# A long chain of engines issued from a written-out table: another order, found with a plan in which TensorE's instruction packets queue behind transfers

## The chip, the cores and the metric

The kernel runs on one core of a Trainium2 chip. The core has five engines that each work through their own list of instructions in order: PE (TensorE, matmuls; its weight loads are listed apart as PEld and overlap the matmuls), DVE (VectorE), ACT (ScalarE), POOL (GpSimd) and SP (SyncE, which here only issues transfers). They wait for one another through semaphores. Sixteen DMA engines carry the transfers. PE writes to PSUM, the others move results from there to SBUF, the on-chip memory; such a move is called an evacuation below. The metric is the device time of one execution in microseconds (us).

## The reference, cut to what matters

One sequence of 2048 positions with 512 channels goes through a state-space layer and an MLP, each with a layernorm ahead and a residual.

```python
def ssm(u, A_re, A_im, B_re, B_im, C_re, C_im, log_dt, Dskip):   # D = 512, N = 128, L = 2048
    dt = exp(log_dt)[:, None]
    logdA = dt * (A_re + 1j * A_im)
    P = exp(logdA[:, :, None] * arange(L))
    K = einsum("dn,dnl,dn->dl", C, P, dt * B).real               # the kernel of the convolution
    y = irfft(rfft(u padded to 2L) * rfft(K padded to 2L))[:L]   # along L, for each channel
    return y + u * Dskip

h  = x + ssm(layernorm(x), ...)
h2 = h + B(layernorm(h))   # B(z) = gelu(layernorm(z) @ w1 + b1) @ w2 + b2
```

B begins with a layernorm of its own; w1 is 512 x 1376 and w2 1376 x 512.

## The kernel before, in words

*The work.* The convolution's K is never formed by L exponentials for each state. Positions are split into blocks, so that K is a product of a table of powers within a block and one across blocks. Both tables come from the parameters by small sums on DVE and POOL, by exponentials and sines on ACT, and by long DVE products:

- The head: loads of the parameters and of u, transposes (L776 to L814), `split` and `restack` (L758 to L765; the transfers `ar<-ar` of 64 KB on SP), the exponentials of `bexps` (L800) and `aexps` (matmuls L1014, ACT L1018). One ACT_TABLE_LOAD (L559) then turns ACT from exponentials to sines.
- The chain: PE makes angles (L1070), ACT their sines (L1074), and DVE multiplies them into the tables (L1081 to L1083, L1089, L1090, and the large products L1041). The layernorm of u is beside it: BN_STATS on DVE (L947, four for each group of rows), and `unorm` (L959).
- K, in two halves: `kgen` (L1115, L1116) is 1024 tiny matmuls, 128x33, that read the tables. The second half reads the products that the chain ends with. A carry of a few rows between neighbouring blocks goes by four transfers on SP (L1136). `kspec` (L1159) takes the K blocks to spectra, which ACT or DVE evacuates.
- The way through memory: the spectra are stored to DRAM (`AK_d<-ar`, 512 KB each, eight of them, called at L1174) and loaded back in another layout (`ar<-AK_d`, eight of 512 KB, L1178), all on SP's queue through the helper `dma` (L577). `fstage` (L991) takes them a stage further on PE. `xspec` (L971) and `fstage` do the same for the input, with no trip through memory.
- `inverse`: products of the spectra (L1207, L1212; DVE or POOL) and matmuls back (L1223); its results are turned by DMA transposes (`turn`, L1229).
- `lead` and `tail` (L1285 to L1350): residual, skip term, the layernorms of the MLP.
- `mlp`: w1 and gelu (PE L1372, ACT L1374), w2 and the output (PE L1394, DVE L1396), and stores of the output. `load_mlp` (L1253 to L1257) loads the weights, `load_small` (L1260 to L1268) the bias b1, as 128x10 and 96x1 single values, and Dskip.

*What sets the order.* Each of 966 pieces of work is only recorded, by `Sched.add`, with what it reads and writes, its costs and the engines that may do it (the evacuations, several sums, the inverse's products and `unorm` have two: ACT or DVE, DVE or POOL). `Sched.run` then goes through the table `ORDER`, 966 numbers written out in the code, and issues the pieces one after the other; a negative number stands for a piece's second engine. So the table sets each engine's order and the choice of engine. While it goes, `run` keeps a plan of times. In this kernel the plan has two effects on what is issued: which of the four PSUM buffers (128x1024 f32) a piece gets, and where filler matmuls (L1488, work without a use) stand, which are put in where the plan sees PE wait. 78 of them are issued.

*Packets in the plan.* PE's instructions come to it in packets, and the plan's class `Ring` holds the transfers under way. At each 256th instruction of PE, `until` says when the next packet has come: before, 3.65 us after the last, and longer by 0.3 of the time in which transfers were under way. The numbers in the plan are the planner's own and no measurement.

Lines of the new kernel are 8 higher than these from L280 on: its L1123 is L1115 here, L1049 is L1041, L955 is L947, L585 is L577, L575 is L567.

Of the kernel before, what the change touches and what calls it, by code (L numbers as in the profile page):

```python
# [15 lines left out]
P = 128  # L16
# [147 lines left out]
class VS(V):  # L164
# [49 lines left out]
]  # L214


FREE = {"PE": 1.3, "ACT": 0.7, "DVE": 0.8, "POOL": 1.4, "SP": 0.7}
WIN, PHASE, ACTIVE = 3.4133, -1.4, 1.25
SWITCH = 0.095


class Clock:
    def __init__(self):
        self.end, self.act, self.warm = PHASE + WIN, 0.0, False

# [31 lines left out]
class Ring:  # L257
# [3 lines left out]
    def add(self, x, y):  # L261
        if y <= x:
            return
# [6 lines left out]
    def until(self, t0):  # L270
        o = 0.0
# [1258 lines left out]
```

## Time and profile before

| what | value |
|---|---|
| three runs | 240.89, 238.55, 242.34 us |
| median | 240.89 us |
| the profiled execution | 238.77 us |
| its span, first to last instruction | 237.0 us |
| mean granted clock of PE | 0.993 |
| DMA | 24.16 MB in 42294 packets |

A row of the profile gives an engine, a line, an operation with its tiles (`ar` is SBUF, `ps` PSUM, `AK_d` the spectra in DRAM, `in_...` the inputs), a count, and busy time. Behind `<-` stands what ended an idle time: an engine with its last operation, a DMA, or `issue`, where the engine waited for nothing that the profile shows. In rows of the timeline the first number is the start, the second the length, and a wait ahead of the row is in brackets. Rows of the list of waits give the sum, the count, and the longest. SPq is SP issuing a transfer. A queue's row gives packets, MB and its share of the time of 16 DMA engines; q8 carries PE's instructions and q1 the kernel's own transfers.

### The profile page before, as it was taken

What the parts mean: (1) busy time and instruction counts of PE and PEld (TensorE: products, weight loads), DVE (VectorE), ACT (ScalarE), POOL (GpSimd) and SP (SyncE); (2) the same over time, 40 slices, a digit from 0 to 9 for tenths busy, and PEclk for the clock granted to TensorE, in tenths of its full rate; (3) what the DMA queues carried; (4) which work ended last, traced back from release to release, by engine and by line L of the source; (5) the groups of instructions that cost most, each with busy time, mean ns of one, the idle gap of its engine ahead of it and who ended that gap; (6) DMA issues with size and microseconds to landing.
All of it is one profiled execution on the core that took longest, in us unless ns stands there. A gap on an engine that the chain in (4) does not pass through costs nothing.

```text
span 237.0 us, 7873 instructions
## 1 busy us (share of the span) xinstructions
PE 208.3 (88%) x3375; PEld 119.2 (50%) x3386; DVE 173.6 (73%) x325; ACT 170.9 (72%) x208; POOL 44.8 (19%) x216
## 2 busy tenths in 40 slices
PE   5195899869998899769999978999999999999993
PEld 3033743426776567445766554565444444444443
DVE  3999898999999875448989978998934757122022
ACT  6998999899999797539989968978547305604700
POOL 6854930000000033008060001601000101000000
PEclk9999799999999999999999999999999999999999
DMA  6972010100000448805898899340933051611203
GB/s 163 222 147 68 25 49 0 47 1 6 3 6 11 116 141 200 301 17 160 265 224 212 223 202 307 68 89 3 175 58 67 3 100 44 144 25 33 55 22 78
DMA packets 42294, 24.16 MB, mean 102 GB/s; under 512 B 25810, under 2 KB 39604, under 8 KB 42260
## 3 DMA queue, kind: packets, MB, share of 16 engines
q1 hardware_dynamic: 41810, 23.34, 41.0%
q8 instruction: 26, 0.43, 0.7%
q10 hardware_dynamic: 450, 0.33, 0.4%
q14 instruction: 8, 0.07, 0.1%
HBM read 9.90 MB, written 6.29 MB: 68 GB/s over the span
## 4 chain that ended last, share of the span: by engine, by line
PE 50%; DVE 17%; ACT 16%; DMA 9%; issue 4%; SPq 2%; ACTq 1%; DVEq 0%
PE ps L1394 16%; PE ps L1372 16%; DMA ar<-AK_d 4%; ACT ar L565 4%; PE ps L991 4%; DVE ar L1041 3%; ACT ar L1018 3%; PE ps L971 3%; ACT ar L800 3%; PE ps L1159 3%; DMA ar<-ar 2%; DVE ar L1081 2%; PE ps L1115 2%; PE ps L1116 2%; PE ps L1223 2%
## 5 line engine op out<-in xcount | busy, mean ns | idle before, releaser
L565 ACT CAST ar<-ps 128x1024 bf16<-128x1024 f32 (+2 forms) x71 | 63.9, 976 | 19.0 <-PE ps L991 5.3
L1374 ACT ACTIVATE ar<-ps,ar 128x512 bf16<-128x512 f32 (+1 forms) x44 | 28.6, 686 | 28.0 <-PE ps L1372 19.2
L1372 PE MATMUL ps<-ar 128*128 128x512 bf16 (+2 forms) x192 | 39.9, 361 | 0.1
L1394 PE MATMUL ps<-ar 128*128 128x512 bf16 (+3 forms) x181 | 39.1, 366 | 0.3
L1074 ACT ACTIVATE ar<-ps 128x1024 bf16<-128x1024 int16 x36 | 34.6, 1047 | 1.8 <-PE ps L1070 1.1
L567 DVE CAST ar<-ps 128x1024 bf16<-128x1024 f32 (+2 forms) x21 | 24.3, 1172 | 13.3 <-PE ps L991 6.8
L1396 DVE TENSOR_TENSOR ar<-ps,ar 128x512 bf16<-128x512 f32 (+1 forms) x17 | 11.0, 657 | 28.5 <-PE ps L1394 28.3
L1372 PEld LDWEIGHTS <-ar 128*128 128x128 bf16 (+1 forms) x192 | 18.8, 100 | 19.4 <-issue 1.2
L1394 PEld LDWEIGHTS <-ar 128*128 128x128 bf16 (+1 forms) x187 | 18.0, 98 | 19.9 <-issue 0.4
L1207 DVE TENSOR_TENSOR ar<-ar 128x2048 bf16<-128x2048 bf16 x21 | 25.4, 1243 | 1.0 <-PE ps L1223 0.9
L1488 PE MATMUL ps<-ar 128*128 128x512 bf16 x73 | 20.5, 419 | 5.8 <-DMA ar<-in_A_u_dram 4.8
L1070 PE MATMUL ps<-ar 128*32 128x512 f16 (+1 forms) x368 | 21.6, 331 | 3.9 <-ACT ar L1074 3.9
L1116 PE MATMUL ps<-ar 128*20 128x33 bf16 x512 | 20.9, 248 | 3.7 <-issue 3.7
L1115 PEld LDWEIGHTS <-ar 128*20 128x20 bf16 x512 | 18.4, 123 | 5.0 <-issue 3.5
L1115 PE MATMUL ps<-ar 128*20 128x33 bf16 x512 | 20.8, 248 | 0.0
L991 PE MATMUL ps<-ar 128*32 128x256 bf16 (+1 forms) x384 | 18.2, 309 | 2.9 <-DMA ar<-AK_d 2.0
L1116 PEld LDWEIGHTS <-ar 128*20 128x20 bf16 x512 | 18.2, 124 | 2.1 <-issue 1.6
L927 POOL TENSOR_TENSOR ar<-ar 128x4 f32<-128x4 f32 (+1 forms) x5 | 5.7, 1145 | 67.9 <-DVE ar L616 58.7
L971 PE MATMUL ps<-ar 128*32 128x512 bf16 x256 | 17.3, 380 | 0.0
L1041 DVE TENSOR_TENSOR ar<-ar 128x2048 bf16<-128x2048 bf16 x14 | 16.2, 1219 | 0.0
L1488 PEld LDWEIGHTS <-ar 128*128 128x128 bf16 x78 | 7.7, 105 | 16.4 <-issue 5.4
L1070 PEld LDWEIGHTS <-ar 128*32 128x32 f16 x368 | 9.9, 98 | 12.0 <-issue 9.3
(113 smaller groups left out, 295.9 us busy)
## 6 DMA issues: line engine op xcount, KB each, us to landing
AK_d<-ar SPq DMA_DIRECT2D x8, 512.0 KB
ar<-AK_d SPq DMA_DIRECT2D x8, 512.0 KB
ar<-in_A_u_dram SPq DMA_DIRECT2D x4, 512.0 KB
out_dram<-ar SPq DMA_DIRECT2D x30, 64.0 KB
ar<-in_B_w_dram SPq DMA_DIRECT2D x4, 344.0 KB
ar<-ar SPq DMA_DIRECT2D x20, 64.0 KB
ar<-in_B_w_dram SPq DMA_DIRECT2D x2, 640.0 KB
ar<-ar SPq DMA_DIRECT2D x8, 48.0 KB
```

The costliest lines, as they stand in the source:

```text
L565: act.copy(out_fn(), in_fn())
L971: pe.matmul(pst(p)[32 * cg:32 * cg + 32, 512 * z:512 * z + 512], lhsT=BD.ap()[:, 32 * f + 2 - 2 * jl:32 * f + 34 - 2 * jl], rhs=un[2 * (2 ...
L991: pe.matmul(pst(p)[64 * h + z:64 * h + z + 32, w * (k + r):w * (k + r) + w], lhsT=T.ap()[:, f, r, z:z + 32], rhs=rhs(f), start=True, stop= ...
L1070: pe.matmul(pst(p)[32 * g:32 * g + 32, 256 * j:256 * (j + n)].rearrange("p (a b) -> p a b", a=n), lhsT=W2[DELTAS.index(d)].ap(), rhs=S2[g] ...
L1074: add("ACT", c_act(1024), lambda e, o_=o_, i_=i_: act.activation(o_(), i_(), ACT.Sin, scale=SINSC), r=[p, TBL], w=[sc[cs]])
L1115: pe.matmul(o, lhsT=Ar.ap()[:, :, d], rhs=Br.ap()[:, :, d], start=True, stop=False, tile_position=(0, 32 * g))
L1116: pe.matmul(o, lhsT=Ai.ap()[:, :, d], rhs=Bi.ap()[:, :, d], start=False, stop=True, tile_position=(0, 32 * g))
L1207: (dve if e == "DVE" else gp).tensor_tensor(pieces(o).rearrange("p z (a r d) -> p a z r d", a=4, r=2), k, x, ALU.mult)
L1372: pe.matmul(pst(p)[:fs, 512 * z + 128 * t0:512 * z + 128 * t1], lhsT=w1s[dc].ap()[:, fc * P:fc * P + fs], rhs=ybuf.ap().rearrange("p (t c) ...
L1374: add("ACT", c_act(512, 1), lambda e, p=p, z=z, fc=fc, fs=fs: act.activation(hT.ap()[:fs, fc, :], pst(p)[:fs, 512 * z:512 * z + 512], ACT. ...
L1394: pe.matmul(pst(p)[:, 512 * z + c0:512 * z + c1], lhsT=hT.ap()[:fs, fc, 128 * t:128 * t + 128], rhs=w2s[fc].ap()[:fs, c0:c1], start=(fc == ...
L1488: pe.matmul(slots[z][:, 0:512], lhsT=identb.ap(), rhs=hs[15].ap(), start=True, stop=True)
```

## The change

The table `ORDER` is another permutation of the same 966 pieces, with other choices of engine for some 60 of them; what each piece computes and what it depends on is unchanged. The plan's model of packets is new, and so the fillers are 66 instead of 78, and some PSUM buffers are others. The pieces that moved, as far as the prediction speaks of them:

- DVE: the last four of the 16 BN_STATS of the input's layernorm stand behind the chain's last product instead of ahead of the chain. A net two of the inverse's products (L1207), a net one of the `unorm` and two scalings go from DVE to POOL; one sum (`den`) comes from POOL; memsets are exchanged between the two, and evacuations between DVE and ACT, both ways.
- PE: the second half of K begins with other groups, and two groups of `kspec` (L1159) that read the carry stand behind the first of them instead of ahead. One group of the inverse (L1223) stands ahead of the first matmul of the MLP.
- SP: the 128x10 bias load stands among the restacks of the head instead of ahead of the first AK_d loads; the four first AK_d stores follow in a row; the AK_d loads stand apart, with stores, a slice of w1 (344 KB), w2's last rows (96 KB) and the carry between them; the last AK_d load stands behind four turns instead of three.

SP's order in the head now, around the bias load:

```order
L1273 DMA ar<-in_A_Dskip_dram 1x4x32
L585 DMA ar<-ar 64x1x512 x2
L1273 DMA ar<-in_B_b_dram 128x10x1
L585 DMA ar<-ar 64x1x512 x4
L1273 DMA ar<-in_A_Dskip_dram 1x4x32 x2
L1144 DMA ar<-ar 12x2048 x4
```

Before, all four Dskip loads came last, behind the restacks and ahead of the carry, and the bias load as the prediction shows it. The diff, with the table cut to a line:

```diff
 ORDER = [
...
 ]
@@
+CUT, EARLY = 0.2, 0.4
@@ class Ring:
     def __init__(self):
-        self.q = [[-100.0, -100.0] for _ in range(6)]
-    def add(self, x, y):
-        if y <= x:
-            return
-        for q in self.q:
-            if q[0] - 0.02 <= x <= q[1] + 0.02:
-                q[1] = max(q[1], y)
-                return
-        min(self.q, key=lambda q: q[1])[:] = [x, y]
-    def until(self, t0):
-        o = 0.0
-        for a, b in self.q:
-            o += max(0.0, min(b, t0 + 5.5) - max(a, t0))
-        return t0 + 3.65 + 0.3 * min(o, 5.5)
+        self.q = []
+    def add(self, a, b, turn):
+        self.q = [(a, b, turn)] + self.q[:9]
+    def until(self, t0, q=None):
+        f = t0 + 1.15
+        for a, b, turn in self.q if q is None else q:
+            if turn:
+                if a < t0 and b > f:
+                    f = max(f, min(b, t0 + 2.05))
+            elif a < t0 - CUT and b - EARLY > f:
+                f = b - EARLY
+        return f + 2.45
+    def late(self, t0, blk):
+        a, b, turn = self.q[0]
+        f = self.until(t0, self.q[:1])
+        return max(0.0, f - blk) if f > t0 + 3.6 else 0.0
@@ Sched.run, a piece of PE
                 while n0 < ipe:
-                    n1 = min(ipe, n0 - (n0 - 192) % 256 + 256)
+                    n1 = min(ipe, n0 - (n0 - 177) % 256 + 256)
                     t = clk.work(t, c * (n1 - n0) / o.ni, o.act / o.cost[0])
                     n0 = n1
-                    if (n1 - 192) % 256 == 0:
-                        t = blk = max(t, ring.until(blk))
+                    if (n1 - 177) % 256 == 0:
+                        t = max(t, ring.until(blk))
+                        blk0, blk = blk, t
@@ Sched.run, a transfer
-                ring.add(a, dma_busy)
+                    ring.add(end, dma_busy, False)
+                d = ring.late(blk0, blk)
+                free["PE"] += d
+                blk += d
@@ load_small
-        add("SP", 0.55, lambda e: nd(b1_bf.ap()[:, 0:10], B_b1[0:1280].rearrange("(fc p) -> p fc", p=P)), w=[b1_bf], byts=8192)
-        add("SP", 0.55, lambda e: nd(b1_bf.ap()[0:96, 10:11], B_b1[1280:1376].rearrange("(p o) -> p o", o=1)), w=[b1_bf], byts=8192)
+        add("SP", 0.6, lambda e: nd(b1_bf.ap()[:, 0:10], B_b1[0:1280].rearrange("(fc p) -> p fc", p=P)), w=[b1_bf], byts=400000)
+        add("SP", 0.55, lambda e: nd(b1_bf.ap()[0:96, 10:11], B_b1[1280:1376].rearrange("(p o) -> p o", o=1)), w=[b1_bf], byts=30000)
```

In the new plan a packet goes out 1.15 us after the last boundary, but behind transfers already issued, takes 2.45 us, and a transfer that is issued later can still delay it (`late`). The bias loads stand in the plan with more bytes, since their values are single; what they load is the same.

More of the change, by code (lines that the diff above doesn't have):

```diff
@@ L328, in run @@
         dma_busy, bulk, ring = 0.0, 4.0, Ring()
-        ipe, blk, md, pst, issued, held = 0, -10.0, 0, 0.0, 0.0, 0.0
+        ipe, blk, blk0, md, pst, issued, held = 0, -10.0, -20.0, 0, 0.0, 0.0, 0.0
         order, seen = [], set()
@@ L396, in run @@
                 bulk = share(a, o.byts / 230e3, dma_busy)
-                ring.add(a, bulk)
+                ring.add(end, bulk, False)
                 o.end = bulk + 0.3
@@ L405, in run @@
                     dma_busy = max(share(end, 2.5, bulk), dma_busy)
+                    ring.add(end - c, dma_busy, True)
                 else:
```

67 rows, old and new, of the table ORDER are left out of this document.

## The prediction

> **What bounds the kernel now.** I read the page first: busy time by engine, the DMA queues, the chain of work that ended last.
>
> ```profile
> PE 208.3 (88%) x3375; PEld 119.2 (50%) x3386; DVE 173.6 (73%) x325; ACT 170.9 (72%) x208; POOL 44.8 (19%) x216
> ```
>
> PE (TensorE) is the busiest, but an 88% share is a mean over stages. So the second view cuts the span where the work changes. The columns are the length, the busy time with the number of instructions for PE, PEld, DVE, ACT and POOL, the granted clock, the busy share of the DMA engines and GB/s.
>
> ```profile
> 36.00:82.00 46.00, 40.20 (x1051) 24.67 (x1044) 44.39 (x92) 43.29 (x51) 0.13 (x1) 1.00 0.10 24
> 82.00:99.70 17.70, 16.88 (x601) 11.92 (x592) 9.89 (x18) 12.64 (x13) 4.37 (x6) 1.00 0.70 201
> 99.70:102.60 2.90, 0.12 (x7) 0.05 (x8) 1.24 (x2) 1.01 (x1) 0.00 (x0) 1.00 0.27 102
> 102.60:134.40 31.80, 30.99 (x817) 20.90 (x816) 28.42 (x28) 28.39 (x31) 9.43 (x4) 1.00 0.75 185
> 134.40:150.50 16.10, 13.40 (x196) 7.85 (x193) 14.04 (x27) 13.16 (x17) 1.45 (x2) 1.00 0.99 249
> 150.50:233.50 83.00, 82.51 (x487) 40.26 (x491) 44.27 (x85) 39.66 (x57) 6.67 (x4) 1.00 0.30 62
> ```
>
> From 36 to 82 us DVE has 44.4 of 46 us: it is the bound, with ACT (43.3) close behind. From 82 on PE is, except in the hole at 99.7. In 134.4 to 150.5 every DMA engine is busy (0.99). The MLP after 150.5 is PE alone, 82.5 of 83.0.
>
> The third view is the waits of PE from 82 to 151 us, with what ended them; the fourth the timeline at the two ends that matter.
>
> ```profile
> PE ps L1116 <- issue: 2.8, 1, 2.8
> PE ps L991 <- DMA ar<-AK_d: 2.0, 2, 1.6
> PE ps L991 <- issue: 0.8, 1, 0.8
> PE ps L1320 <- ACT ar L565: 0.3, 1, 0.3
> ```
> ```profile
> 34.60 1.28 ACT L559 ACT_TABLE_LOAD   x1
> 75.48 5.77 DVE L1041 TENSOR_TENSOR ar<-ar 128x2048 bf16<-128x2048 bf16 x5
> 81.19 1.05 PE L1159 MATMUL ps<-ar 32*128 32x256 bf16 x31 [0.78 <-DMA ar<-ar]
> 82.17 0.27 PE L1115 MATMUL ps<-ar 128*20 128x33 bf16 x4
> 102.55 0.23 PE L1116 MATMUL ps<-ar 128*20 128x33 bf16 x1 [2.78 <-issue]
> 150.96 0.60 PE L1372 MATMUL ps<-ar 128*128 128x256 bf16 x4
> ```
>
> DVE's last chain products end at 75.48 + 5.77 = 81.25; 0.92 later, at 82.17, PE begins the second half of the kernel's K, which reads them. In 82 to 151 PE waits 2.8 + 0.8 = 3.6 us for "issue", which is neither data nor a buffer.
>
> **What the issue waits are.** The page counts 26 packets of the instruction queue, 0.43 MB, and PE's two rows 3375 + 3386 = 6761 instructions: 260 for each packet, so a packet carries about 256. Now the DMA view of two stretches around the hole, and PE's rate and stall in a stretch without traffic.
>
> ```profile
> q8 instruction: 26, 0.43, 0.7%
> ```
> ```profile
> q1 hardware_dynamic: 488, 1.79, 92.1%
> ```
> ```profile
> q1 hardware_dynamic: 57, 0.18, 19.3%
> q8 instruction: 1, 0.02, 2.5%
> ```
> ```profile
> 88.01 1.93 SPq L1265 DMA_DIRECT2D ar<-in_B_b_dram  x1
> 90.06 0.70 SPq L577 DMA_DIRECT2D AK_d<-ar  x1
> 90.93 4.44 SPq L577 DMA_DIRECT2D ar<-AK_d  x4
> ```
> ```profile
> 68.00:72.00 4.00, 4.00 (x170) 3.47 (x173) 4.00 (x10) 3.49 (x5) 0.00 (x0) 1.00 0.02 4
> 90.00:92.00 2.00, 2.00 (x55) 1.21 (x49) 0.72 (x3) 1.03 (x2) 0.87 (x1) 1.00 0.55 64
> ```
> ```profile
> 73.29 0.25 PE L1116 MATMUL ps<-ar 128*20 128x33 bf16 x1 [0.91 <-issue]
> ```
>
> In 94 to 100 us (the first of the two) the only queue with packets is the kernel's data, at 92%: no packet of instructions in 6 us. In 100 to 102.5 (the second) one comes, as the data thins out, and PE goes on at 102.55. The data are the four AK_d loads issued in a row from 90.93 to 95.37, 2 MB. The bias load of 1280 values issued at 88.01 delayed them: in 90 to 92 the engines moved 64 GB/s at a share of 0.55. The stall at 72.4 (0.91) is of another kind: DMA share 0.02 ahead of it, but 343 instructions in 4 us, 256 in 3.0. So there are two limits, a packet that queues behind transfers and a rate of packets.
>
> [...]
>
> **The change, part by part.** *DVE ahead of the chain.* The order of DVE (VectorE) before, at the end of the head; BN_STATS are statistics of input rows, L1081 (later) the chain:
>
> ```order
> L616 TENSOR_SCALAR ar<-ar 128x16
> L947 BN_STATS ar<-ar 128x6 x3
> L755 TENSOR_TENSOR ar<-ar 128x512
> L616 TENSOR_SCALAR ar<-ar 128x16
> L947 BN_STATS ar<-ar 128x6
> L626 TENSOR_TENSOR ar<-ar 128x8
> L733 TENSOR_SCALAR ar<-ar 64x32
> ```
>
> The order of DVE now, at the end of the chain; L1049 are its products, L955 the same BN_STATS, L575 evacuations:
>
> ```order
> L624 TENSOR_SCALAR ar<-ar 128x16
> L634 TENSOR_TENSOR ar<-ar 128x512
> L1049 TENSOR_TENSOR ar<-ar 128x2x2x512 x2
> L575 CAST ar<-ps_66 128x4x256
> L955 BN_STATS ar<-ar 128x6
> L575 CAST ar<-ps_65 128x2x8x64
> L955 BN_STATS ar<-ar 128x6 x2
> L575 CAST ar<-ps_65 128x2x8x64
> L955 BN_STATS ar<-ar 128x6
> ```
>
> Four BN_STATS moved from ahead of the chain to behind its last product. Their row (28 to 36 us) and those of the evacuations:
>
> ```profile
> L947 DVE BATCH_NORM_STATS2 ar<-ar 128x6 f32<-128x512 bf16 x6 | 3.8, 682 | 0.0
> L567 DVE CAST ar<-ps 128x1024 bf16<-128x1024 f32 (+2 forms) x21 | 24.3, 1172 | 13.3 <-PE ps L991 6.8
> L565 ACT CAST ar<-ps 128x1024 bf16<-128x1024 f32 (+2 forms) x71 | 63.9, 976 | 19.0 <-PE ps L991 5.3
> ```
>
> 3.8 / 6 = 0.63 each, 2.5 us off a saturated engine. Other exchanges ahead of the chain's end nearly cancel: one evacuation (1.17) leaves DVE, another comes, two small sums and a scaling come, memsets leave. I take 0.5 more, partly through the table load at 34.60 coming earlier. The chain's end moves by -3.0, to 78.25, and the K start to 79.2. Bounds: -1.0, if ACT, which has 46 - 43.3 = 2.7 us idle in this stretch and little of it at the end, sets the chain; -3.5.
>
> *PE after the chain.* Now the tiny K matmuls of the second half come first; the two L1159 groups of 16 that waited for the carry (0.78) follow. From 82.17 to 134.4 PE took 52.2 us, of it 2.78 + 0.82 + 0.34 (the smaller AK_d wait, 2.0 - 1.6) and 0.3 waits: 48.0 work. The L1159 groups add 1.2 (L1159's row above, 1.05 for 31, and the next start); of the L971 pairs three go ahead of the chain's end and two come behind it, which I cost at nothing together. 49.2 then.
>
> *The transfers.* SP's order before, around AK_d (the K spectra's way through memory; L1136 is the carry):
>
> ```order
> L1136 DMA ar<-ar 12x2048 x4
> L577 DMA AK_d_69<-ar 128x8x256 x2
> L577 DMA AK_d_68<-ar 128x8x256
> L577 DMA ar<-in_B_w_dram 96x512
> L1265 DMA ar<-in_B_b_dram 128x10x1
> L577 DMA AK_d_68<-ar 128x8x256
> L577 DMA ar<-AK_d_69 128x2048
> L577 DMA ar<-AK_d_68 128x2048 x2
> L577 DMA ar<-AK_d_69 128x2048
> L1136 DMA ar<-ar 12x2048 x4
> ```
>
> and now:
>
> ```order
> L1144 DMA ar<-ar 12x2048 x4
> L585 DMA AK_d_69<-ar 128x8x256
> L585 DMA AK_d_68<-ar 128x8x256 x2
> L585 DMA AK_d_69<-ar 128x8x256
> L585 DMA ar<-AK_d_68 128x2048
> L585 DMA ar<-in_B_w_dram 96x512
> L585 DMA ar<-AK_d_69 128x2048
> L585 DMA ar<-in_B_w_dram 128x1376
> L1144 DMA ar<-ar 12x2048 x4
> L585 DMA ar<-AK_d_68 128x2048
> L585 DMA AK_d_70<-ar 128x8x256
> L585 DMA ar<-AK_d_69 128x2048
> ```
>
> The bias load is gone to the head, among the restacks; what it costs there falls before the chain, where the DMA share is 0.10. The loads are apart, but a 344 KB slice of w1 now stands between them. New issue waits lie between 0 and the present 3.6; a row of four loads gave those, and two loads and the slice are 0.7 of its bytes, with gaps. I take 1.5. For evacuations exchanged between ACT and DVE I add most of one late evacuation, 0.8 (0 to 1.17). So 49.2 + 2.3 = 51.5, and this stage ends at 130.7, 3.7 before 134.4.
>
> *From there to the MLP* I keep the 16.1 us, its wait of 1.6 for AK_d included: its transfers start as much earlier, since before it the DMA engines stand idle a quarter of 31.8 us. That is 8 us of cover for 3.7; without it the gain is lost up to 3.7. *MLP*: one group of 32 small L1223 matmuls, 1.0 us,
>
> ```profile
> 151.56 1.00 PE ps L1223 x32
> ```
>
> now stands ahead of the first L1372 matmul, among filler matmuls: -1.0. Against the sum I allow 0.3 for a clock or a buffer lost. Filler matmuls (78 to 66) fill waits and are costed at nothing.
>
> **Sum**: -3.0 (chain) + 1.2 (L1159) - 4.2 (old waits) + 2.3 (new waits) = -3.7; -1.0 + 0.3 gives -4.4. The profiled execution took 238.77 us, 1.8 of it outside its span of 237.0, so 234.4. The median shown is 240.89, 1.0089 times as long; 234.4 x 1.0089 = 236.4, 1.9% below it. All times below are on the median's scale.
>
> **The rivals.** (1) Packets wait as before, at other places: the rate limit stays, as at 72.4, and a load is ahead of most packets. New waits 3.6 + 0.8 instead of 2.3: 236.4 + 2.1 = 238.5. For it: K matmuls are as dense as ever; against: the 2.78 had no second like it. [...] (2) ACT sets the chain's end, or the last AK_d loads hold the start of the MLP: about 2.5 of the gain goes, 238.9. For it: ACT's 43.3 of 46, and the 0.99 in 134.4 to 150.5. (3) No new waits at all: 234.0. (4) Slower: stores, loads and the w1 slice now meet every packet of the dense K stretch, rather than one. PE issues 601 + 592 instructions in 17.7 us there, 256 in 3.8. A transfer of 512 KB ahead takes about 2 us (1.79 MB in 6 us). A packet that needs 3.0 + 0.9 = 3.9 at 72.4 then needs 5.9, 2.1 too long; PE starts some six blocks from 79 to 103: 12.6 of waits for 1.5, 236.4 + 11.1 = 247.5. It undoes the gain from 4.4 + 1.5 = 5.9 us of issue waits, three such blocks, on. For it: four stores now follow in a row; against: 82 to 99.7 already has a share of 0.70, with six stores and loads, and of issue waits only the 0.8.
>
> **How the numbers follow.** Forecast 0.42, own range 234 to 238.5; rival (1) 0.18, (2) 0.10, (3) 0.10, (4) 0.20, from 241 to 250. Predicted is 236.4. The range from 232.5 to 245 leaves out 0.15 of (4) and a little below (3). Within 2%, which is about what a measurement of this kernel can tell from no change, is 236.1 to 245.7. Faster: all of (3) and 0.19 of the forecast's, 0.29; slower: 0.14, most of (4); same: 0.57.
>
> **What would show it.** Right: the last L1049 product ends near 78.3, K's second half starts near 79.2, the waits list has no issue wait over 1.5 us after 79 and the first MLP matmul is near 147. The chain's step is wrong if DVE shows waits for L1082's sines (ACT, L1074 before) or the end stays above 80; the packets' step if issue waits after 79 sum to over 3; the transfers' step if PE's wait for AK_d before the MLP grows beyond 1.6. Rival (4) shows as issue waits near 2 us at every packet from 79 to 103.

## The result, and the profile after

The changed kernel took 238.34 us, the median of 20 runs (235.96 to 242.29), beside 239.57 us for the kernel before in 20 runs taken with it. The ratio is 0.9937, 95% interval 0.9908 to 0.9966: 0.6% faster, 1.5 us, where 1.9% was forecast. The profiled execution took 237.72 us with a span of 235.9, against 238.77 and 237.0 before, so the two traces differ by 1.1 us. (The profiled executions of five experiments below, e1, e2, e6, e8 and e9, were longer than most other runs of the same kernel; of these the durations and the starts up to 85 us are read, and later rows with care.)

First the changed kernel's page, engines' busy time, and three of its windows, cut as before.

```profile
PE 204.8 (87%) x3362; PEld 119.1 (50%) x3374; DVE 175.2 (74%) x320; ACT 172.1 (73%) x208; POOL 53.2 (23%) x221
```
```profile
36.00:82.00 46.00, 40.23 (x1033) 24.47 (x1035) 45.23 (x83) 44.19 (x51) 0.42 (x2) 1.00 0.06 12
...
99.70:102.60 2.90, 2.77 (x98) 2.52 (x100) 1.26 (x4) 2.25 (x3) 0.00 (x0) 1.00 0.17 33
102.60:134.40 31.80, 28.70 (x716) 18.36 (x712) 26.99 (x26) 28.26 (x31) 12.92 (x4) 1.00 0.80 208
```

DVE is busier from 36 to 82 us (45.23 of 46, before 44.39). The four BN_STATS that were moved stood ahead of this window before (between 31.65 and 35.12 us) and stand behind it now, so they never were part of its 44.39. The hole at 99.7 is gone (PE 2.77 of 2.90, before 0.12), but PE has 28.70 us of work in the next 31.8 us where it had 30.99. Now the waits of PE from 80 to 151 us, and the timeline at the places that were shown of before.

```profile
PE ps L999 <- DMA ar<-AK_d: 2.1, 2, 1.6
PE ps L1123 <- issue: 1.7, 2, 1.2
PE ps L1231 <- issue: 0.9, 2, 0.6
```
```profile
35.59 1.28 ACT L567 ACT_TABLE_LOAD   x1
...
79.08 2.36 DVE L1049 TENSOR_TENSOR ar<-ar 128x2048 bf16<-128x2048 bf16 x2
...
149.87 1.07 PE L1231 MATMUL ps<-ar 64*128 64x128 bf16 x32
150.87 3.40 PE L1380 MATMUL ps<-ar 128*128 128x256 bf16 x22
```

The table load comes 1.0 us later than before (34.60), the last chain product ends at 79.08 + 2.36 = 81.44 where it ended at 81.25, and 78.25 was forecast. Other executions with the changed kernel's head (e6, e7, e13 and e14 below) end the chain between 81.16 and 81.88, and those with the head of the kernel before (e3 to e5) between 81.20 and 81.57, so the two ends can't be told apart. K's second half starts at 81.50, 0.7 earlier (82.17 before), only because it no longer stands behind the carry. The 1.1 us are found at the MLP: its first matmul is at 150.87, before at 150.96, with the 1.0 us group of L1231 ahead of it rather than behind.

So the question was where the 2.5 us went that BN_STATS had given back to DVE. The timeline of DVE and of POOL in the head of the changed kernel:

```profile
17.37 2.28 DVE L644 TENSOR_SCALAR ar<-ar 128x512 f16<-128x512 f32 x1
...
28.88 1.26 DVE L624 TENSOR_SCALAR ar<-ar 128x16 int32<-128x16 int32 x1
...
33.89 0.80 DVE L634 TENSOR_TENSOR ar<-ar 128x8 f32<-128x8 f32 x1
```
```profile
19.23 0.15 POOL L898 MEMSET ar<- 128x16 f32 x2
...
28.83 1.27 POOL L634 TENSOR_TENSOR ar<-ar 128x512 f32<-128x512 f32 x1
...
32.30 2.38 POOL L624 TENSOR_SCALAR ar<-ar 128x1024 int32<-128x1024 int32 x2 [0.64 <-DVE ar L622]
```

The same three forms of DVE instruction take 0.43, 0.28 or less, and 0.16 us where POOL is still. Each long one ends just behind the POOL work that runs beside it: 19.65 behind memsets that end at 19.38, 30.14 behind 30.10, 34.69 behind 34.68. The memsets are a row of 59 that begins at 16.65. Against the short forms that is 1.85 + 0.98 + 0.64 = 3.5 us. The same stretch of the kernel before, DVE and then POOL:

```profile
13.84 2.14 DVE L616 TENSOR_SCALAR ar<-ar 128x512 f32<-128x512 f32 x2
...
20.78 6.02 DVE L947 BATCH_NORM_STATS2 ar<-ar 128x6 f32<-128x512 bf16 x10
...
31.65 1.88 DVE L947 BATCH_NORM_STATS2 ar<-ar 128x6 f32<-128x512 bf16 x3
```
```profile
31.89 1.27 POOL L626 TENSOR_TENSOR ar<-ar 128x512 f32<-128x512 f32 x1 [2.12 <-DVE ar L616]
33.13 0.66 POOL L616 TENSOR_SCALAR ar<-ar 128x512 int32<-128x512 f32 x1
```

The three BN_STATS at 31.65 are among the four that were moved. POOL's sum and scaling ran beside them, and they kept their 0.6 us apiece; the 128x16 scaling stood at 34.24, with POOL still, and took 0.28. BN_STATS was not only work: it was what DVE did while POOL worked. The kernel before had a stretched row too: at 13.84 two scalings, which take 0.42 us each elsewhere, took 2.14 together beside its memsets (13.52 to 15.50). Net of these 1.3 us, the changed kernel's three rows cost 2.2, nearly what BN_STATS gave back.

Whether DVE's time counts is seen where the chain starts, at DVE's first instruction that reads what ACT made behind its table load. Here it is before and in the changed kernel, and then a wait of ACT in the head of the changed kernel:

```profile
36.55 1.42 DVE L642 SCALAR_TENSOR_TENSOR ar<-ar 128x512 f32<-128x512 f32 x2 [0.64 <-ACT ar L649]
```
```profile
37.54 1.42 DVE L650 SCALAR_TENSOR_TENSOR ar<-ar 128x512 f32<-128x512 f32 x2 [0.21 <-ACT ar L657]
```
```profile
21.02 0.72 ACT L657 ACTIVATE ar<-ar 128x512 f32<-128x512 f32 x1 [1.05 <-DVE ar L634]
```

Before, DVE was there first and waited 0.64 us for ACT; taking work off DVE ahead of that place could not bring the chain forward by itself (e1 below tries it). Now the chain starts 1.0 us later: ACT has one evacuation more (0.99 us) and has waited 1.05 us for DVE's sums, which stand behind the long scaling at 17.37.

### The profile page after: what moved, and what is told of

Same layout as the page of the kernel before. It is cut to its first block, busy times and chain, and to the rows that moved or that the text cites. A ratio compares the mean times of both kernels' runs of the same rounds, so it can differ in the third digit from the quotient of the medians.

```text
span 235.9 us, 7856 instructions
## 1 busy us (share of the span) xinstructions
PE 204.8 (87%) x3362; PEld 119.1 (50%) x3374; DVE 175.2 (74%) x320; ACT 172.1 (73%) x208; POOL 53.2 (23%) x221
## 4 chain that ended last, share of the span: by engine, by line
PE 52%; DVE 7%; DMA 5%; issue 2%; ACT 2%; SPq 0%; DVEq 0%
PE ps L1380 16%; PE ps L1402 16%; PE ps L1231 4%; PE ps L999 3%; DMA ar<-AK_d 2%; DVE ar L1049 2%; DMA AK_d<-ar 2%; PE ps L1123 2%; PE ps L979 2%; ACT ar L573 2%; PE ps L1124 2%; PE ps L1496 2%; DVE ar L1215 1%; PE ps L1167 1%; DVE ar L575 1%
## 5 line engine op out<-in xcount | busy, mean ns | idle before, releaser
L1380 PE MATMUL ps<-ar 128*128 128x512 bf16 (+2 forms) x192 | 40.0, 361 | 0.0
L575 DVE CAST ar<-ps 128x1024 bf16<-128x1024 f32 (+3 forms) x23 | 25.2, 1108 | 8.0 <-PE ps L999 3.7
L1380 PEld LDWEIGHTS <-ar 128*128 128x128 bf16 (+1 forms) x192 | 18.8, 100 | 18.9 <-issue 0.7
L1215 POOL TENSOR_TENSOR ar<-ar 128x2048 bf16<-128x2048 bf16 x5 | 20.3, 4069 | 32.3 <-DVE ar L1220 20.9
L1496 PE MATMUL ps<-ar 128*128 128x512 bf16 x60 | 16.7, 408 | 9.9 <-DMA ar<-in_A_u_dram 8.9
L1215 DVE TENSOR_TENSOR ar<-ar 128x2048 bf16<-128x2048 bf16 x19 | 23.3, 1255 | 2.6 <-PE ps L1231 1.7
L1078 PE MATMUL ps<-ar 128*32 128x512 f16 (+1 forms) x368 | 21.1, 331 | 3.8 <-ACT ar L1082 3.5
L1123 PE MATMUL ps<-ar 128*20 128x33 bf16 x512 | 20.3, 248 | 2.2 <-issue 1.7
L1124 PE MATMUL ps<-ar 128*20 128x33 bf16 x512 | 20.5, 249 | 0.0
L1049 DVE TENSOR_TENSOR ar<-ar 128x2048 bf16<-128x2048 bf16 x14 | 16.4, 1221 | 0.2
L1231 PE MATMUL ps<-ar 64*128 64x128 bf16 x448 | 15.4, 217 | 1.2 <-issue 0.9
L979 PE MATMUL ps<-ar 128*32 128x512 bf16 x256 | 16.3, 380 | 0.0
```

What stands on the lines that cost most here:

```text
L575: dve.tensor_copy(out_fn(), in_fn())
L1078: pe.matmul(pst(p)[32 * g:32 * g + 32, 256 * j:256 * (j + n)].rearrange("p (a b) -> p a b", a=n), lhsT=W2[DELTAS.index(d)].ap(), rhs=S2[g] ...
L1123: pe.matmul(o, lhsT=Ar.ap()[:, :, d], rhs=Br.ap()[:, :, d], start=True, stop=False, tile_position=(0, 32 * g))
L1124: pe.matmul(o, lhsT=Ai.ap()[:, :, d], rhs=Bi.ap()[:, :, d], start=False, stop=True, tile_position=(0, 32 * g))
L1215: (dve if e == "DVE" else gp).tensor_tensor(pieces(o).rearrange("p z (a r d) -> p a z r d", a=4, r=2), k, x, ALU.mult)
L1231: pe.matmul(pst(p)[:, 512 * h + 128 * k:512 * h + 128 * k + 128], lhsT=o[z].ap()[rows, k, r, :], rhs=TP[w].ap()[rows, f0 // 2 + k, :], sta ...
```

## The experiments

My theory after the result: *the chain's end did not come earlier because DVE's short instructions now stand beside POOL and wait for it.* The rivals: ACT, with its later table load, holds the chain; the packets' waits ate the gain behind the chain; the lead's time was lost to the transfers. Numbers in the diffs are pieces of the table. Ratios are to the kernel before, with 95% intervals.

**e1, BN_STATS alone.** The kernel before, with only its last four BN_STATS and two small sums that need them behind the chain.

```diff
- 549, 550, 551, 552 (BN_STATS), 555, 557 ahead of the chain
+ ... behind 405, the first evacuation after the last L1041 product
```

> The kernel before, with the four BN_STATS of the second half's layernorm (0.63 us each) and the two small sums that read them moved behind the chain's last product and one evacuation. Theory of the prediction (DVE's work ahead of the chain is on the path): the last product ends 2.5 us earlier, near 78.8, and the total falls by 2 to 2.5 us. Theory now (ACT's exponentials and its table load set the start of the chain, so DVE work ahead of it is beside the path): the table load stays at 34.6, the last product at 81.25, both within 0.4; the total is the same or up to 1 us longer, since the statistics now stand between evacuations of the spectra.

Its timeline: DVE, with the chain's start and the last products, and POOL.

```profile
32.15 1.24 DVE L616 TENSOR_SCALAR ar<-ar 128x16 int32<-128x16 int32 x1
...
36.38 1.42 DVE L642 SCALAR_TENSOR_TENSOR ar<-ar 128x512 f32<-128x512 f32 x2 [1.84 <-ACT ar L649]
...
75.14 5.77 DVE L1041 TENSOR_TENSOR ar<-ar 128x2048 bf16<-128x2048 bf16 x5
```
```profile
31.79 1.57 POOL L626 TENSOR_TENSOR ar<-ar 128x512 f32<-128x512 f32 x1 [2.12 <-ACT ar L1018]
```

2.5 us of work left DVE, and the last product ends at 80.91 instead of 81.25: 0.3 earlier, no more than executions of one head differ. A scaling of 0.22 to 0.28 us took 1.24, because it met the POOL sum that BN_STATS had covered; a 64x32 one took 0.64 instead of 0.17. That is 1.4 of the 2.5 us. The other 1.1 went into a wait: at the chain's start DVE stood 1.84 us waiting for ACT, where it had stood 0.64, since ACT's table load, at 34.42 (34.60), came only 0.2 earlier. So in the kernel before ACT sets the chain's start, not DVE, as the second theory above has it. The step of my sum that takes 2.5 us from DVE's work to the chain's end falls by this alone. The time decides nothing here: the ratio is 1.0045 with a wide interval (0.9966 to 1.0124), and the medians of all runs, 236.58 us and 238.46 for the kernel before, stand the other way round.

**e2, e8, e9, e10: POOL beside DVE.** In e2 the row of 59 memsets of POOL in the changed kernel is put later, in e8 all 16 BN_STATS are put back as cover in the head, in e9 the three overlaps shown are taken apart, and e10 is e9 with an evacuation of the head (0.99 us) given back from ACT to DVE.

```diff
 e2:  - 124 (POOL, 59 memsets) early      + 124 just ahead of 125
 e8:  - BN_STATS in several places        + 546 to 552 in one row behind 152; POOL's scalings 29, 30 behind 26
 e9:  + 124 right behind 108, 2.4 us earlier; DVE's scalings 40, 122 behind 86; POOL's scaling 29 behind 26
 e10: + as e9;  71 on DVE, not ACT
```

> The kernel after, with one piece of POOL (59 small memsets, 16.65 to 19.37 us) moved behind six other pieces of POOL, so that it no longer runs beside DVE's scaling at 17.37 us. Theory now (the scaling took 2.28 us instead of 0.42 because of those memsets, and the restacks, the exponentials and the table load wait for it): the scaling takes 0.4 to 0.5 us, the restack at 20.41 is issued near 18.6, the table load is 1.0 to 1.5 us earlier (34.1 to 34.6 instead of 35.59), the chain's end 0.7 to 1.5 earlier, the total 0.5 to 1.5 us shorter. Rival (the scaling is long by itself, or ACT is full without it): the scaling stays over 1.5 us, or the table load stays within 0.4 of 35.59 though it is short.

> The kernel after with all 16 BN_STATS in one row in the head, the four that the change moved among them, and two scalings of POOL moved up so that POOL's work from 24 to 33 us runs beside them. It puts 2.4 us of DVE work back ahead of the chain. Cover theory (beside POOL's memsets and scalings DVE's short operations are stretched, 0.97, 0.64 and 0.35 us of it in the kernel after, and BN_STATS are not): these three go back to their short times, so the last chain product ends 0.4 us later than 81.44, within 0.5. Rival, the prediction's sum (only the work counts): it ends 2.4 us later, near 83.8. In both the spectra's first store, at 84.37 in the kernel after, loses the statistics ahead of it.

> The kernel after, with four pieces of the head moved so that POOL no longer runs beside DVE's short operations: POOL's 59 memsets start 2.5 us earlier, beside subtractions and products of DVE, two small scalings of DVE go behind the f16 scaling that was stretched to 2.28 us, and one scaling of POOL comes 1.6 us earlier. The four BN_STATS stay behind the chain. Overlap theory (the prediction's 2.9 us less DVE work ahead of the chain's end is there, and 3.5 us of stretched operations ate it): the three stretched operations return to 0.43, 0.2 and 0.1 us, DVE is ready for the chain at or before 36.2 (37.54 in the kernel after), the table load comes at 34.0 to 34.6 (35.59), the last product ends 1.0 to 1.7 us earlier (79.7 to 80.4), and the first MLP matmul and the total follow by 0.8 to 1.7. Rival (the stretching only moves to other operations, as when the memsets alone were moved later): the last product stays within 0.5 of 81.44.

> The same, and the one evacuation of the head that the change gave to ACT (0.99 us there) is back on DVE (1.14 us). Overlap theory with ACT as the next bound: the table load is 0.5 to 1.0 us earlier again (33.2 to 34.0), and the last product ends 0.3 to 1.0 earlier than with the overlap removed alone (79.0 to 80.0); the total 1.5 to 2.5 below the kernel after. Rival (DVE is the bound of the head, so the evacuation costs there what it saves on ACT): table load and chain end are the same as with the overlap removed alone, or later, within 0.4.

The timeline of e8, DVE and ACT:

```profile
23.33 9.58 DVE L955 BATCH_NORM_STATS2 ar<-ar 128x6 f32<-128x512 bf16 x16
...
33.02 0.28 DVE L624 TENSOR_SCALAR ar<-ar 128x16 int32<-128x16 int32 x1
```
```profile
33.69 0.30 ACT L657 ACTIVATE ar<-ar 128x8 f32<-128x8 f32 x1 [2.60 <-DVE ar L650]
...
37.76 1.28 ACT L567 ACT_TABLE_LOAD   x1
```

BN_STATS does cover: the 16 take 0.60 us apiece beside POOL's work, and the scaling is back to 0.28 us (the one at 17.37, which e8 leaves where it is, still takes 2.28). But the last product ends at 84.17 (81.81 + 2.36), near the 83.8 of the rival and not the 81.8 of the cover theory. The small sums behind the long row come late, ACT waits 2.60 us for them, and the table load slips to 37.76. The ratio, from four runs, is 1.0107 (0.9996 to 1.0218). In e8 cover in the wrong place cost more than it saved, and it cost through ACT, whose exponentials waited those 2.60 us for DVE's sums. In e2 the first scaling is back to 0.43 and the table load comes to 34.08, yet the chain ends at 81.65, where 0.7 to 1.5 us earlier than 81.44 was expected, because other instructions now meet POOL's work (a 128x8 sum takes 1.61 us, a 128x16 one 1.17): ACT came 1.5 us earlier, and DVE, which starts the chain at 37.73 without a wait, held it alone. 0.996 (0.993 to 0.9989), as the changed kernel itself.

The timeline of e9, again DVE, POOL and ACT:

```profile
17.37 0.43 DVE L644 TENSOR_SCALAR ar<-ar 128x512 f16<-128x512 f32 x1
...
27.27 1.40 DVE L634 TENSOR_TENSOR ar<-ar 128x8 f32<-128x8 f32 x2
...
35.83 1.42 DVE L650 SCALAR_TENSOR_TENSOR ar<-ar 128x512 f32<-128x512 f32 x2 [0.34 <-ACT ar L657]
...
77.39 2.36 DVE L1049 TENSOR_TENSOR ar<-ar 128x2048 bf16<-128x2048 bf16 x2
```
```profile
15.03 1.50 POOL L891 MEMSET ar<- 128x1 f32 x44
```
```profile
33.87 1.28 ACT L567 ACT_TABLE_LOAD   x1
```

Here the memsets run beside 128x512 sums, which they do not slow (0.69 us), and the scaling takes 0.43. Not every overlap is gone: two 128x8 sums take 1.40 us at 27.27, beside a sum of POOL. But ACT no longer waits for DVE ahead of its table load, which comes 1.7 us earlier, and so do the chain's start and its end, at 79.75. Two later kernels with this head, e12 and e15, end the chain at 80.07 and 79.74. The ratio, from six runs, is **0.9858 (0.9806 to 0.991)**: faster than the kernel before, and probably than the changed one, whose interval (0.9908 to 0.9966) it just touches. Against the kernel before the end is 1.5 us earlier, half of the forecast 3.0. Only places of POOL's and DVE's small work were changed, and with them the plan's fillers. In e10 the chain ends at 81.39 again, with 0.9985 (0.9952 to 1.0018), where I expected it earlier still: with one evacuation more on DVE, ACT waits 0.61 and 0.37 us for DVE's sums, its table load comes at 34.72, and the gain is gone. So DVE with its stretched instructions holds the head of the changed kernel, directly (e2) and through the sums that ACT waits for (1.05 us at 21.02; also e8 and e10); for that kernel the theory stands. The rival with ACT is half right: in the kernel before ACT sets the chain's start (e1), and only what lets both come earlier, as e9 does, reaches the chain's end.

**e3, e5, e6: the transfers.** e3 is the kernel before with the bias load in the head, e5 the kernel before with two of its four AK_d loads moved behind stores and the carry, e6 the changed kernel with its first four AK_d loads in a row.

```diff
 e3: - 164 (128x10 bias load) ahead of the AK_d loads   + 164 behind 120, in the head, and its memset 162 ahead of it
 e5: + AK_d load 409 behind the third store, 408 (and 412, 413, which need it) behind the carry
 e6: + 408, 390, 409 right behind the first load; the w2 rows behind them
```

> The kernel before, with the 128x10 bias load alone moved to the head (between the restacks, with its memset). Theory: without it the four AK_d loads start about 2 us earlier and the engines are free earlier, so the packet asked for near 94.3 comes about 2 us earlier: the wait of 2.78 us before 102.55 falls to about 0.8, and, as PE is the bound of this stretch, the total falls by 1.0 to 2.0 us. Rival one (the packet waits for the four loads in a row, whenever they start): the loads only move, a wait of over 2 us stays. Rival two (the stretch from 134 to 150 us is held by transfers, not by PE): the wait shrinks, the total stays within 0.5 us.

> The kernel before with its first four AK_d loads apart: the first right behind the third store (ahead of w2's last rows and of the bias load), two where they were, the last behind the carry, with the one fstage group that reads it behind it. The bias load stays where it was. Queue theory (the 2.78 us come from a packet behind 2 MB of loads in a row): the issue wait before 102.55 falls under 1.2 us, since at most 1 MB stands in a row. Rate theory (dense matmuls, whatever the transfers): a wait of over 2 us stays near that place. For the total: if PE's waits before 134 us reach the end, the first MLP matmul comes 1.5 us or more earlier and the total falls by 1.5; if the stages behind 134 us are held by DVE, ACT and transfers, the total stays within 0.7.

> The kernel after with its first four AK_d loads moved together again, right behind the fourth store, as the kernel before has them (the bias load stays in the head). Queue theory: the issue waits of 1.23 and 0.42 us at 94 and 99 grow to 2.5 us or more together, at one place. Rate theory: they stay near 1.7 in sum. The total: up to 1.5 us longer if PE's waits there reach the end, within 0.7 if not.

The waits of PE from 80 to 151 us in e5:

```profile
PE ps L991 <- DMA ar<-AK_d: 4.5, 3, 1.8
PE ps L991 <- issue: 1.4, 1, 1.4
```

In e3, without the bias load, the four AK_d loads are issued from 89.17 us on, before from 90.93 (89.80 in e4, which has the bias load in its old place), and PE waits 0.8 us for AK_d where it waited 2.0 (1.9 in e4). But the issue waits are 2.2 and 1.6, so 3.8 where they were 3.6, and the ratio is 1.0024 (0.9995 to 1.0053): the bias load was not the cause of these waits that I made it. With the loads apart the issue waits fall to 1.4, but those for AK_d rise from 2.0 to 4.5, and the first L1372 matmul comes at 153.08 instead of 150.96: 1.012 (1.0012 to 1.0227), from four runs. The loads moved apart were themselves late: in e5 one is issued at 87.08 us, two at 95.55 and the last at 104.80, where before all four were issued from 90.93 to 95.37. e6, the reverse on the changed kernel, gives 2.6 of issue and 3.2 of AK_d waits and 0.9998 (0.9952 to 1.0044): not told from the changed kernel.

**e11, e12: where the packets' borders fall.** I then held that an issue wait depends on which instruction is the 256th. Both are e9 with tiny matmuls ahead, which shift the borders; they add work without a use.

```diff
+ 20 (e11) or 14 (e12) matmuls of 128x32 ahead of the first filler
```

> The kernel with no overlap in the head, which the profiled run shows with issue waits of 1.6, 0.7 and 1.4 us after 80 us, and 20 small extra matmuls (40 instructions of PE, 32 columns each, read by nobody) ahead of its first filler matmul, where PE waits 7.8 us for a load. They shift every boundary of 256 instructions against the work by 40 instructions, to where they stand in the kernel with the evacuation on DVE, whose issue waits after 80 us were 0.7. Alignment theory (whether a packet's request meets a transfer or a dense stretch is set by where the boundary falls): issue waits after 80 us sum to under 1.5 instead of 3.7, the chain's end stays at 79.75 within 0.5, and the total is 0.5 to 2 us below that kernel's. Rival (the sum is set by the traffic and the rate, wherever the boundaries are): 3 us or more of issue waits stay, the total within 0.5.

> The same with 14 small extra matmuls (28 instructions), which puts the boundaries where they stand in the kernel after from 80 us on. Alignment theory: issue waits after 80 us as in the kernel after, 2 to 2.8, at the same places in the work; the total between the kernel with no overlap and the one with 20. Rival: as with 20, the same as without any.

e12 had waits of 1.2 and 0.4 at the same borders as the changed kernel, and e11 had others, which looked like support. Ratios 0.9884 (0.9846 to 0.9921) and 0.9911 (0.987 to 0.9952): neither is told from e9's. In e11 PE's granted clock fell behind 36 us; the window with its columns as above:

```profile
36.00:44.00 8.00, 7.09 (x60) 2.04 (x63) 7.83 (x15) 6.44 (x7) 0.00 (x0) 0.50 0.14 33
```

In the same window the clock was 1.00 in e9 and 0.79 in e12, with as few fillers; why it fell is open. The chain then ended at 81.32, so e9's gain there was gone, but the time stayed below that of the kernel before, as the K stage behind it waited only 1.4 us for issue and 1.0 for AK_d. The runs of the next group decide on the borders.

**e4, e7, e13, e14, e15: the lead and the MLP's start.** In the changed kernel PE's last lead matmul ends 1.7 us earlier (142.41, before 144.12), but the MLP begins hardly earlier. e4 is the kernel before with only the L1223 group ahead of the MLP; e7 the changed kernel with an evacuation of ACT behind the three activations of the tail; e13 the changed kernel without the fillers ahead of the transposes L1358; e14 is e13 with that evacuation behind the copies as well; e15 is e14's edit on e9.

```diff
 e4:  + 743 (L1223 group) ahead of 674 (first L1372 matmul)
 e7:  + 476 (ACT, 128x1024) behind the activations of 646 and 648
 e13: + no fillers ahead of 642, 644, 647, 649 (L1358)
 e14: + as e13; 476 behind 650
```

> The kernel before, with only the one group of 32 small L1223 matmuls moved ahead of the first matmul of the MLP, as in the kernel after. Theory (the filler matmuls ahead of the MLP cover it): the MLP ends 1.0 us earlier, the total is 0.8 to 1.1 us shorter, which would be the whole gain of the change. Rival (it delays the first MLP matmul by as much): the total within 0.3 us.

> The kernel after with one evacuation of ACT (the last AK_d stage of the second half, 146.36 to 147.37 us) moved behind the three layernorm activations of the first tail, as it would stand behind them if the MLP came first. Theory (the kernel after has its last lead matmul 1.7 us earlier than the kernel before, and gives 0.9 of it back here, since the activation at 147.26 was ready at 146.4): the three activations, the first MLP matmul (150.87) and the end come 0.7 to 1.0 us earlier. Rival (something else, such as the transposes or the weights, holds the MLP): the first MLP matmul stays within 0.3.

> The changed kernel without the ten filler matmuls that stand ahead of and between the first transposes of the MLP (L1358). In the changed kernel these begin at 148.45, right behind eight fillers, while the first activation of the tail (147.26, some 0.75 each) is there at 148.0. Theory 'ACT's queue holds the start of the MLP': the last transposes still wait for the third activation, which ends at 149.49; the first transposes begin at 148.0, but the L1231 group stays at 149.9 and the first L1380 matmul at 150.9, both within 0.2. Theory 'the fillers hold it': everything behind them moves by 0.4, L1380 to 150.4. A third way: PE has worked less by then, its granted clock falls and L1380 comes later than 151.1. Total within 0.3% of the changed kernel in each case.

> As the run before (no fillers ahead of L1358), and ACT's last evacuation of L999 (128x1024, 0.99 us) moved from ahead of the tail's three activations to behind the two copies of their transposes. Theory 'ACT's queue': the activations begin right behind DVE's L650 (146.18 + 0.16 in the changed kernel), near 146.5 instead of 147.26, the group at about 149.1 and L1380 at 150.1, 0.8 earlier, measured from the end of the lead's last L1297 matmul (142.41 in the changed kernel, 8.46 ahead of L1380; then 7.7). Rival: DVE's sums or PE's own order set it, and L1380 stays 8.3 to 8.5 behind that matmul.

> The last run's edit on top of the kernel in which POOL and DVE no longer overlap in the head (ratio 0.986). If the two gains add: last chain product near 79.8, L1380 7.7 behind the last L1297 matmul, ratio to the kernel before 0.980 to 0.984. If the time behind the chain is set by transfers alone, L1380 comes no earlier than 150.3 and the ratio stays at 0.985 to 0.988.

e4: the group at 150.10, the MLP at 151.10, 0.14 later than before with 1.0 us less to do; span 236.3 (237.0), ratio 0.997 (0.9935 to 1.0005). e7: 1.0014 (0.9964 to 1.0064), no gain. To see why, the timeline of the changed kernel between the lead and the MLP, PE and then ACT, and last of e14, ACT and PE:

```profile
146.51 2.10 PE L1496 MATMUL ps<-ar 128*128 128x512 bf16 x8 [0.37 <-ACT ar L573]
148.45 0.39 PE L1358 MATMUL ps<-ar 128*128 128x128 bf16 x4
```
```profile
144.45 2.92 ACT L573 CAST ar<-ps 128x1024 bf16<-128x1024 f32 x3 [0.72 <-PE ps L999]
147.26 2.23 ACT L1350 ACTIVATE ar<-ar 128x512 bf16<-128x512 bf16 x3
```
```profile
144.26 2.23 ACT L1350 ACTIVATE ar<-ar 128x512 bf16<-128x512 bf16 x3
...
147.43 1.07 PE L1231 MATMUL ps<-ar 64*128 64x128 bf16 x32 [0.49 <-ACT ar L573]
148.43 2.78 PE L1380 MATMUL ps<-ar 128*128 128x256 bf16 x20
```

In the changed kernel DVE's last sum (L650) is ready at 146.34, and the activations wait for ACT's three casts until 147.26; behind them PE's transposes wait for eight fillers. e14 takes both away. Counted from the end of the last L1297 matmul (142.41, e14 140.23) the activations come after 4.03 instead of 4.85 us, as expected; but the MLP's first L1380 comes after 8.20 instead of 8.46, where 7.7 was expected, since the group now waits 0.49 for a PSUM buffer that ACT evacuates. e7 had its activations after 4.04 and its L1380 after 8.24: the fillers and its own moved evacuation ahead of the copies gave the gain back. In e13 the activations stay at 4.85, as they should if ACT holds them, and behind the 2.00 us that PE was idle its granted clock was 0.50: the L1231 group took 1.89 instead of 1.07 us. e13's timeline there, and its window (PE's busy time, granted clock, DMA share, GB/s):

```profile
148.05 1.89 PE L1231 MATMUL ps<-ar 64*128 64x128 bf16 x32
```
```profile
148.00:150.00 2.00, 2.00 (x35) 0.50 0.82 220
```

e13 gave 0.9954 (0.9899 to 1.0009); e14's four runs, 235.59 to 241.84, give no ratio; e15 gave 0.9898 (0.9853 to 0.9943), not told from e9 (0.980 to 0.984 was expected if the two gains add), with the same 1.89 us group. So three things stand behind one another, ACT's queue, the fillers and a buffer, and these edits got about 0.25 us out of the stretch from the lead to the MLP.

These runs also settle the borders. Up to 146 us the instructions of the changed kernel, e7, e13 and e14 are the same on PE, with the same borders. The waits of PE from 80 to 136 us in e13, and then in e14:

```profile
PE ps L1123 <- issue: 0.9, 2, 0.5
PE ps L999 <- DMA ar<-AK_d: 0.8, 2, 0.6
PE ps L1231 <- issue: 0.5, 1, 0.5
```
```profile
PE ps L999 <- DMA ar<-AK_d: 2.6, 3, 1.6
```

In the order changed kernel, e7, e13, e14 the four executions waited 2.6, 0.2, 1.4 and 0.2 us for issue and 2.1, 3.1, 0.8 and 2.6 for AK_d, and their last L1297 matmul ends anywhere from 140.23 to 142.97. In the first three the issue waits stand at the same instructions (the only one of e14, 0.2, stands elsewhere), but their sizes belong to the execution. The theory of the borders as the cause of the sizes falls, and with it any reading of 1 or 2 us of these waits from a single profile, mine of e3 and e5 included; for e5 the ratio speaks. What did come back is the long wait of the kernel before: in e4, the same order up to there, it is 3.0 us, at the same matmul as the 2.8, while the longest of the four executions here are 1.2, 0.2, 0.5 and 0.2. Whether the row of loads makes it is not shown: e6, with the loads in a row again, has 1.6 at most.

## Why the prediction was right and wrong, by its own steps

**The chain, -3.0: wrong, and the step that failed.** The work taken off DVE was as costed, four BN_STATS of 0.61 to 0.69 us. What failed is "3.8 / 6 = 0.63 each, 2.5 us off a saturated engine" as a move of the end, for two reasons. The work stood where DVE was not the bound: the 44.4 of 46 us are those from 36 to 82, the four BN_STATS stood before 36, and at 36.55 DVE waited 0.64 us for ACT; in e1, without them, it waited 1.84. And the instructions left behind did not keep their durations: beside POOL three of them took 3.5 us more, 1.7 of which e9 got back at the chain's end. In place of -3.0 the end did not move (81.44, before 81.25). The sign that I named for it, an end above 80, is there. The lower bound that I gave, -1.0 by ACT's idle time, was no bound: that time was taken from the stretch behind the chain's start, and no row of an instruction stretched beside POOL was in my sum, although the kernel before had one at 13.84. That one evacuation leaves DVE was right, but it put 0.99 us on ACT ahead of its table load, so this came 1.0 us later and not earlier. The sum also kept the 0.92 us from the chain's end to K's start, although it had moved away the carry's groups that filled them: 0.06 is left of it, and this chance gain hides part of the miss. Of the 3.3 us between the span that the sum gives (237.0 - 4.4 = 232.6) and 235.9, the chain's end makes 3.2, this gap -0.9 and the K stage 1.4; the allowance of 0.3 takes up nearly all of the rest.

**PE after the chain, +1.2 for L1159 and new waits of 2.3 for the old 4.2.** The K stage started at 81.50 and its successor at 134.37, 52.9 us, of which 4.9 are waits (1.7 + 0.9 + 2.1 + 0.2): 48.0 of work, as before, and no 1.2 more. A group of 16 of L979 takes 1.1 us (three went ahead of the chain's end and two came behind it, which I cost at nothing together); counting that net group would cancel the 1.2. The rows of the two stretches have 176 L971 matmuls before and 160 of L979 now, as this needs; it was not tried by itself. The waits of 2.3 were mis-sized against this execution, but the same code showed 2.2 to 4.7 for issue and AK_d together in four executions, so that no single profile could have decided on 2.3. By my own sign this step held: no issue wait over 1.5, 2.6 in sum. The direction, fewer long issue waits and more waits for loads, is what the traces show: the longest issue wait fell from 2.8 to 1.2, and AK_d waits of 2.1 us came ahead of 134 where 0.3 stood. That the bias load's delay of the loads makes the long wait is not borne out: in e3 the loads came 1.8 us earlier, and 3.8 us of issue waits stayed.

**134.4 to 150.5 kept at 16.1: about right, by other means.** From 134.37 to the first MLP matmul it took 16.5 with the 1.0 us group in it, 15.5 without. Its wait of 1.6 for AK_d is gone, and most of that went to ACT's queue and to fillers, as the changed kernel's timeline and e14 show. PE waited for no transfer there.

**The L1223 group, -1.0: right.** It is nearly all of the 1.1 us between the two profiles, and e4 alone has a span shorter by 0.7, though its ratio is not told from 1.

**The rivals.** Rival (1) gave nearly the time that was measured, 238.5 against 238.34, but not the cause: it kept the gain of the chain and let the waits take the rest. Rival (2), 238.9, had the right place, the chain, and half the cause: ACT sets its start in the kernel before (DVE waits 0.64 us for it, in e1 1.84); in the changed kernel DVE and ACT come almost together (0.21 us of wait), ACT held up by DVE (1.05 us at 21.02). Rival (4) did not come: issue waits of 2 us at every packet are in none of these traces. What was missing was a rival in which DVE's own instructions grow.

## What to carry to other kernels

Before an instruction is moved off a busy VectorE, look at what GpSimd does at that moment: if the moved instruction was one that GpSimd doesn't slow (here BN_STATS, 0.60 to 0.63 us beside it), it was cover, and what moves up beside GpSimd may take much longer (five to ten times here: 0.43 to 2.28 us, and 0.16 to 1.61 in e2). Then look at the place where the gain should arrive: an engine that waits there for another has nothing to give, however busy it is later (DVE in e1, 1.84 us for ACT). A saturated engine's time need not be the sum of durations read at other places (a 128x16 scaling took 0.28 us in one and 1.26 in another); check the same form of instruction with and without its neighbour. And run the same code several times in the profile before 1 or 2 us of waits for instructions or transfers are read as an effect of an edit (here the issue waits of four executions of the same code were up to 2.4 us apart).

## What the runs showed of the hardware that was not expected

**GpSimd beside VectorE.** In the changed kernel's head a 128x512 scaling, a 128x16 scaling and a 128x8 sum of DVE ran until POOL's work beside them had ended (0.43 to 2.28, 0.28 to 1.26, 0.16 to 0.80 us); BN_STATS kept 0.60 to 0.63 beside POOL's work (e8, and before), and the 128x512 f32 sums of DVE 0.69 beside the memsets. So POOL's memsets, whose rows have no input, held the 128x512 scaling and did not slow the 128x512 sums, while the 128x8 sum at 33.89 was held beside a scaling of POOL, which has one. The scaling of 17.37 was held through 58 short memsets in a row (17.39 to 19.38 us) and ended behind the last, at 19.65. Why some forms are held and others are not, no run shows.

**The clock.** In e13 PE was idle for 2.00 and 0.30 us up to 147 us, and the granted clock was 0.50 from 148 to 150 (0.68 from 150 to 152); behind waits of 1.18, 0.31 and 0.28 us it was 0.50 from 148 to 150 in e15 too, and with waits of 1.17, 0.31 and 0.49 it was 1.00 in e14. So nearly the same gaps stood beside half the clock in one execution and the full clock in another. What makes the difference is not shown.

**Waits for instructions**, summed from 80 to 136 us, differ between executions of the same code by up to 2.4 us (0.2 to 2.6).
